# Rearranging the input half of an S4D + token-mixer kernel: block-diagonal input rows in one set, MLP modulations side by side, columns spread over steps 10 to 30

## The chip, the cores and the metric

The kernel runs on one core of one Trainium2 chip. The metric is device time in microseconds (us) of one execution: the median of several runs. One further execution was recorded by the hardware profiler, and all rows below come from it.

## The reference

Input `x` is 2048 tokens by 448 channels. A condition vector `c` gives six modulation vectors of 448 values; the block then is a long convolution (S4D) and a token-mixing MLP, each behind a layer norm:

```python
mod = (silu(c) @ w_mod).reshape(1, 6, 1, 448)
sa, ca, ga, sb, cb, gb = (mod[:, k] for k in range(6))
h = layernorm(x) * (1 + ca) + sa
K = 2 * einsum("dn,dnl->dl", C, exp(A * dt * l)).real        # 448 x 2048 kernel, 256 modes
y = irfft(rfft(h, 4096) * rfft(K, 4096))[:2048] + h * D_skip # along the tokens
x = x + ga * y
h = layernorm(x) * (1 + cb) + sb
x = x + gb * (gelu(layernorm(h).T @ w1 + b1) @ w2 + b2).T
```

## The kernel before, in words

TensorE (PE) computes everything that is a sum: the S4D kernel `K` from its 256 modes, the Fourier transforms as two-stage products with tables, and the MLP. ScalarE (ACT), VectorE (DVE) and GpSimd (POOL) feed it. The order of PE, ACT, DVE and POOL is the program's own order (manual schedule). The order of SyncE (SP), which issues most DMAs, is the program's only until `first.close()`, at step 8; after that a scheduler orders it.

**Steps and windows.** The S4D kernel is made in 56 steps `s` of half a group of 16 channels. In a step (`st_step`) ACT takes `ab`, three sines and cosines (L644 to L649), POOL makes two products `G` (L651, L652) and, two steps ahead, the tile `m` (L630, L632 in `st_mag2`), DVE four products `E` (L653 to L657), and PE the next phases (`st_phase`, L603) and 128 small products into `kg` (`st_kgen`, L678). A step is recognised in the trace by its `ab` (L644), and "step 8" below is the moment at which that instruction starts. Ahead of every eighth step stands a `window(s)`: logs and exponentials on ACT under another function table (`logs`, `angle`), with sixteen exponentials `mag` (L614). Eight steps and the window behind them are called a cycle: steps 0 to 8 the first cycle, 8 to 16 the second, and so on. From step 32 on the cycles carry only the generation and the products of the second half; at 422 us the MLP begins, whose matmuls fill PE to the end.

**What is hung into the steps.** Lists `dve` and `act` hold closures that are run at fixed points (`flush`), `late[s]` holds loads, and tables set how much of other work a step takes along:

- `u_stats(r)`: mean and variance of 128 tokens of x, sixteen times (L494, L495). `x_load` brings x in by POOL's DMA queue.
- `modulation(k, ...)`: one of the six modulation vectors, as four matmuls (L481) whose weights `w_mod` (784 KB each) were loaded before, copied out by ACT (L485). 1, 2 and 3 run in steps 2 to 7, 0 in the window of step 8, 4 and 5 in the window of step 16.
- `u_norm`, `u_rows(n)`: the first transform stage of x, "rows". 32 calls with two matmuls each out of 32 partitions into 64 columns (L525), one DVE product each by `mod[1]` (L528), and for every second call a DMA of 448 KB into `yu_d` (L530). They run in window 8, in steps 8 to 15 and in window 16. Tile `yt` has three buffers.
- `u_cols(k)`: the second stage, "columns". 32 calls with one matmul (L557) of what was read back from `yu_d` (L548), an output on DVE or ACT (L564, L566), and DMAs to `us_d`. They run from step 17 to 31.
- `chain(q)`, q = 1, 2, 3: elementwise work of 128 channels' parameters, cut into pieces by `yield`; `more(n)` runs n pieces. `pace` sets how many per step, `WPACE` how many per eighth of a window. A chain stops at `"logs"` until ACT has run `logs` in a window. Its results go to DRAM (`pars`, L378) and are read back by `load`.

Of the kernel before, what the change touches and what calls it, by code (L numbers as in the profile page):

```python
# [11 lines left out]
F32 = mybir.dt.float32  # L12
# [27 lines left out]
def dft_tables():  # L40
# [16 lines left out]
    t["WU"] = np.tile(w1.transpose(1, 2, 0).reshape(32, 64), (4, 1))  # L57
# [45 lines left out]
    t["S2"] = su.reshape(2, 4, 8, 2, 32 * P).transpose(3, 0, 2, 1, 4).reshape(P, 32 * P)  # L103
# [113 lines left out]
def tile_adaln_s4d_mixer(ctx, tc, i, out):  # L217
# [6 lines left out]
    yu_d = dram.tile([2, 32, 2, 8, 4, D], F32, name="yu_d")  # L224
    us_d = dram.tile([2, 32, P, DC], F32, name="us_d")
    v_d = dram.tile([32, P, D], F32, name="v_d")
    x2_d = dram.tile([L, D], F32, name="x2_d")

# [9 lines left out]
    with ExitStack() as es:  # L238
# [27 lines left out]
        def par_load(q):  # L266
            n = min(P, D - P * q)
            raws[q] = {}
            for nm in ("A_C_real", "A_C_imag", "A_log_A_real", "A_A_imag"):
                raws[q][nm] = qp.tile([P, N], F32, tag=nm, name=nm, bufs=2)  # L270
                nc.sync.dma_start(raws[q][nm][0:n], i[nm][P * q : P * q + n])
# [40 lines left out]
        wu = xp.tile([P, 64], F32, name="wu")  # L312
        wms = {}

        def wm_load(k, tile, eng=nc.sync):
            wms[k] = tile
            eng.dma_start(wms[k], i["w_mod"][:, k * D : (k + 1) * D].rearrange("(q p) d -> p q d", p=PP))
# [11 lines left out]
        def wm_slot(k):  # L329
            w = wm0.rearrange("p k d -> p (k d)")[0:PP]  # L330
            return w[:, 4 * D * (k % 4) : 4 * D * (k % 4 + 1)].rearrange("p (q d) -> p q d", q=4)

        late = {
            2: lambda: wm_load(2, wm_slot(2), G),
            3: lambda: wm_load(3, wm_slot(3), G),
            5: lambda: wm_load(0, wm_slot(0), G),
            6: lambda: [
# [3 lines left out]
            9: lambda: nc.sync.dma_start(svt, i["SV"]),  # L343
            10: lambda: [s2_load(0), s2_load(1)],
            11: lambda: [s2_load(2), s2_load(3)],
            12: lambda: wm_load(4, xt[0:PP, 0:4]),
            13: lambda: wm_load(5, xt[0:PP, 4:8]),
# [14 lines left out]

        def chain(q):

# [7 lines left out]
            def split(src, places):  # L372
                hl = qp.tile([P, 2, N], F32R, tag="hl", name="hl", bufs=3)[0:n]
                V.tensor_copy(hl[:, 0], src)
                yield
                tt(hl[:, 1], src, hl[:, 0].bitcast(F32), ALU.subtract)
                for k, v in places:
                    nc.sync.dma_start(pars[q][v, k, 0:n], hl.bitcast(F32))  # L378
# [25 lines left out]
            stt(s, t, -80 * math.log(2.0) / 2.0**80, s, ALU.mult, ALU.add)  # L404
            yield
            stt(s, ya, 0.5, s, ALU.mult, ALU.add)
            yield
            ts(s, s, ldt2[0:n, q : q + 1], None, ALU.add)
# [4 lines left out]
            ts(ph, aim, dt4[0:n, q : q + 1], None, ALU.mult)  # L413
            yield
            ts(u, ph, MAGIC, MAGIC, ALU.add, ALU.subtract)
            yield
            tt(ph, ph, u, ALU.subtract)
# [3 lines left out]
            ts(u, ph, 128.0, MAGIC, ALU.mult, ALU.add)  # L421
            yield
            ts(u, u, MAGIC, None, ALU.subtract)
            yield
            stt(p64, ph, 128.0, u, ALU.mult, ALU.subtract)
# [3 lines left out]
            ts(xa, xa, 4 * i2p, -0.5, ALU.mult, ALU.add)  # L429
            yield  # L430
            ts(u, cr, 0.0, 0.5, ALU.is_ge, ALU.subtract)
            yield
            tt(xa, xa, u, ALU.mult)
            yield
            ts(u, ci, 0.0, 0.5, ALU.is_ge, ALU.subtract)
            yield
            stt(xa, xa, 0.5, u, ALU.add, ALU.mult)
            yield
            stt(xa, ph, 63.0, xa, ALU.mult, ALU.add)
            yield  # L440
            ts(u, xa, MAGIC, MAGIC, ALU.add, ALU.subtract)
            yield
            tt(xa, xa, u, ALU.subtract)
            yield
            yield from split(xa, [(2, 0)])
        def logs(root=False):
# [7 lines left out]
            if root:  # L454
                S.activation(rs, mv[:, :, 1], AF.Ln, bias=eps_t)
                S.activation(rs, rs, AF.Exp, scale=-0.5)
# [19 lines left out]
        def modulation(k, *halves):  # L476
            if 0 in halves:
                pmods[k] = pms.tile([P, D], F32, tag="ms", name="pm")
            for h in halves:
                for q in (2 * h, 2 * h + 1):  # L480
                    T.matmul(pmods[k], scb[:, q], wms[k][:, q], start=q == 0, stop=q == 3)  # L481
            if 1 not in halves:
                return
            pm = pmods.pop(k)
            act.append(lambda: S.activation(mod[k], pm, AF.Copy, bias=1.0 if k in (1, 4) else 0.0))  # L485
# [11 lines left out]
        def u_scale():  # L497

            tt(nm, rs, rs, ALU.mult)
# [5 lines left out]
        yts = {}  # L505

        def u_norm(R):
            for r in (2 * R, 2 * R + 1):
                if R > 2:
                    S.activation(xt[:, r], xt[:, r], AF.Identity, bias=nm[:, r : r + 1], scale=rs[:, r : r + 1])  # L510
                    continue
                G.tensor_scalar(xt[:, r], xt[:, r], rs[:, r : r + 1], nm[:, r : r + 1], ALU.mult, ALU.add)

        def u_rows(n):

            R, g = divmod(n, 4)
            gp, gl = divmod(g, 2)
            if gl == 0:
                yts[R, gp] = xp.tile([P, 2, D], F32, tag="yt", name="yt", bufs=3)
            if g == 1 and 2 <= R < 7:  # L520
                act.append(lambda: u_norm(R + 1))
            pm = pms.tile([P, D], F32, tag="ms", name="pu")
# [841 lines left out]
```

## Time and profile before

| | |
|---|---|
| runs | 715.73, 719.15, 719.76 us; median 719.15 |
| profiled execution | 720.78 us, of which the trace's span is 719.0 |
| busy | PE 88%, DVE 63%, ACT 61%, POOL 38% of the span |
| mean granted TensorE clock | 0.921 |
| step 0, 8, 16, 24, 32 start at | 28.05, 98.48, 155.38, 205.67, 255.88 us |
| MLP | 422 us to the end |

Shares of busy time are averages over stages with different limits. PE is the bound of the MLP; in the stages before it no engine is full, and what counts there is which wait ends last in a step. The granted clock is read by stretch: 1.00 is full, 0.50 half speed, at which every matmul takes about twice as long.

### The profile page before, as it was taken

To read this page: it belongs to the slowest core of one execution; us is meant where nothing else is said; L and a number is where in the kernel's file an instruction comes from. 1 tells how busy PE (TensorE), PEld (TensorE's weight loads), DVE (VectorE), ACT (ScalarE), POOL (GpSimd) and SP (SyncE) were. 2 spreads that over 40 slices of the span, in tenths; PEclk is the share of its full clock that TensorE was granted. 3 is DMA by queue.
4 is the path that set the end of the run, shared out by engine and by line. 5 is a ranking of instruction groups with operands and counts; after the bars stand their busy time and mean duration, and the time that the engine had idled before them with its cause. 6 is when DMAs were issued, how large, how long until landed. Compare 5 with 4: busy or idle time off the path is not lost. (4 is left out here: it accounts for less than half of the span.)

```text
span 719.0 us, 18288 instructions
## 1 busy us (share of the span) xinstructions
PE 632.4 (88%) x7204; PEld 456.4 (63%) x7204; DVE 453.2 (63%) x875; ACT 438.7 (61%) x876; POOL 273.6 (38%) x328
## 2 busy tenths in 40 slices
PE   0659889979989888799888949999999999999997
PEld 0335335434535556566565617778999999999996
DVE  7469879679778668586684548778622263334441
ACT  5847588887987789989883549787522242222220
POOL 6486437528737787878785600000000000000000
PEclk9868857988998889999899959999999999999999
DMA  7795464266888635535236989974585436655540
GB/s 169 207 191 131 162 192 138 113 229 179 244 227 248 204 92 133 149 100 154 70 102 181 285 245 266 239 195 113 174 231 146 148 109 172 173 155 154 156 139 26
DMA packets 101635, 121.19 MB, mean 169 GB/s; under 512 B 13066, under 2 KB 87422, under 8 KB 101422
## 3 DMA queue, kind: packets, MB, share of 16 engines
q1 hardware_dynamic: 100014, 113.16, 55.2%
q0 software_dynamic: 1536, 6.87, 4.4%
q8 instruction: 57, 0.93, 0.6%
q14 instruction: 28, 0.23, 0.1%
HBM read 84.64 MB, written 34.87 MB: 166 GB/s over the span
## 5 line engine op out<-in xcount | busy, mean ns | idle before, releaser
L202 ACT CAST whi<-w 128x896 fp32r<-128x896 f32 x64 | 59.7, 938 | 131.4 <-PE o L1331 84.7
L651 POOL TENSOR_TENSOR G<-mag,gs 128x512 f32<-128x512 f32 x56 | 71.9, 1284 | 92.4 <-ACT gs L647 92.1
L211 DVE TENSOR_TENSOR wlo<-w,whi 128x896 fp32r<-128x896 f32 x64 | 68.0, 1087 | 40.3 <-ACT whi L202 31.0
L603 PE MATMUL xg<-tab,lph 64*128 64x512 f32 x112 | 68.8, 617 | 25.9 <-ACT xg L649 8.0
L1196 PE MATMUL acc<-h3h,whi 128*128 128x448 f32 x224 | 83.3, 372 | 0.1
L1197 PE MATMUL acc<-h3l,whi 128*128 128x448 f32 x224 | 81.9, 366 | 0.0
L1331 PE MATMUL o<-ul,whi 128*128 128x448 f32 x224 | 81.3, 363 | 0.0
L1330 PE MATMUL o<-uh,whi 128*128 128x448 f32 x224 | 81.2, 362 | 0.0
L1198 PE MATMUL acc<-h3h,wlo 128*128 128x448 f32 x224 | 80.9, 361 | 0.0
L1332 PE MATMUL o<-uh,wlo 128*128 128x448 f32 x224 | 80.6, 360 | 0.0
L678 PEld LDWEIGHTS kg<-E,G 128*32 128x32 f32 x3584 | 59.8, 119 | 32.3 <-issue 16.4
L603 PE MATMUL xe<-tab,lph 64*128 64x512 f32 x112 | 67.8, 609 | 12.2 <-ACT gs L648 10.2
L678 PE MATMUL kg<-E,G 128*32 128x64 f32 x3584 | 69.8, 235 | 2.2 <-issue 1.5
L652 POOL TENSOR_TENSOR G<-mag,gs 128x512 f32<-128x512 f32 x56 | 71.7, 1280 | 0.0
L653 DVE TENSOR_TENSOR E<-m,xe 128x512 f32<-128x512 f32 x56 | 38.3, 683 | 40.8 <-ACT xe L646 31.8
L632 POOL TENSOR_TENSOR m<-mag,w 128x512 f32<-128x512 f32 x56 | 59.9, 1070 | 6.0 <-DVE E L657 1.5
L1334 DVE SCALAR_TENSOR_TENSOR y<-o,b,mod 128x448 f32<-128x448 f32 x16 | 10.9, 684 | 80.3 <-PE o L1332 80.3
L644 ACT ACTIVATE ab<-xe 128x512 f32<-128x512 f32 x56 | 33.7, 601 | 30.3 <-PE xe L603 16.1
L1196 PEld LDWEIGHTS acc<-h3h,whi 128*128 128x128 f32 x224 | 42.3, 189 | 13.8 <-ACT h L1252 6.3
L603 PE MATMUL xe<-tab,lex 64*128 64x512 f32 x56 | 31.7, 575 | 18.8 <-POOL dsk L468 17.2
L614 ACT ACTIVATE mag<-xe 128x512 f32<-128x512 f32 x56 | 35.5, 634 | 19.7 <-PE xg L603 14.0
L603 PEld LDWEIGHTS xg<-tab,lph 64*128 64x128 f32 x112 | 24.3, 217 | 36.3 <-issue 10.3
(229 smaller groups left out, 1486.1 us busy)
## 6 DMA issues: line engine op xcount, KB each, us to landing
w<-in_B_w_dram SPq DMA_DIRECT2D x64, 224.0 KB
w<-in_B_w_dram SPq DMA_DIRECT2D x32, 448.0 KB
yu_d<-yt SPq DMA_DIRECT2D x16, 448.0 KB
yi<-yu_d SPq DMA_DIRECT2D x32, 224.0 KB
us_d<-uo SPq DMA_DIRECT2D x16, 448.0 KB
u<-us_d SPq DMA_DIRECT2D x32, 224.0 KB
v_d<-vt SPq DMA_DIRECT2D x32, 224.0 KB
vt<-v_d SPq DMA_DIRECT2D x16, 448.0 KB
```

The lines of the kernel that those rows point to most:

```text
L211: eng.tensor_tensor(lo, w, hi.bitcast(F32), ALU.subtract)
L603: T.matmul(out[k], lhs[r], rhs[r], start=start, stop=stop)
L632: G.tensor_tensor(m2, me, w[:, :, None].to_broadcast([P, GD, 32]), ALU.mult)
L651: G.tensor_tensor(Gt[:, 1], mg_, v32(sg), ALU.mult)
L652: G.tensor_tensor(Gt[:, 0], mg_, v32(cg_), ALU.mult)
L678: T.matmul(kgs[g][32 * q : 32 * q + 32, m], Gt[:, c, d], E[:, c, d], start=h == 0 and c == 0 and m == 0, stop=h == 1 and c == 1, skip_grou ...
L1196: nc.tensor.matmul(acc[f], hi[:, fs], h3h[:, r], start=r == 0, stop=False)
L1197: nc.tensor.matmul(acc[f], hi[:, fs], h3l[:, r], start=False, stop=False)
L1198: nc.tensor.matmul(acc[f], lo[:, fs], h3h[:, r], start=False, stop=r == 15)
L1330: nc.tensor.matmul(o, hi[:, ks], uh[kh][:, k], start=kh == 0 and k == 0, stop=False)
L1331: nc.tensor.matmul(o, hi[:, ks], ul[kh][:, k], start=False, stop=False)
L1332: nc.tensor.matmul(o, lo[:, ks], uh[kh][:, k], start=False, stop=kh == 1 and k == 6)
```

## The change

All of it lies ahead of the MLP. Line numbers of the changed kernel are about 30 higher (L603 is L633, L481 is L495, L525 is L556, L557 is L587, L678 is L708, L464 is L479, L651 is L681, L378 is L396).

1. Rows. The table `WU` becomes block diagonal, 128 by 128. `u_rows` is called 16 times, with two matmuls each out of 64 partitions into 128 columns; the DVE products stay 32, the DMAs 16. All run in window 8, nothing of them in the steps or in window 16. The first four `u_norm` are on DVE, the other twelve on ACT, six rows ahead.
2. Modulations. 1 and 2 are whole in steps 6 and 7, 0 in the window of step 8; 3, 4 and 5 are computed together in steps 27 and 30, each in 32 output columns, and spread over the partitions through DRAM (`mod_d`). `w_mod` for 1, 2 and 0 is loaded by SP in `late[5]`, no longer by SP and POOL at steps 0 to 5.
3. Columns: one each in steps 10 to 14, one or two in steps 16 to 22 and 24 to 30, three each in windows 16 and 24. `yu_d` is read from step 9 on; `us_d` is written for every second column.
4. Chains. The first half of chain 1 is in window 0, its second half in window 8 and on POOL (`fuse` splits a three-operand instruction in two). Windows take up to 32 pieces, steps at most two and none before step 10. All chains store to `pars` by POOL's queue. The parameters of chain 1 are loaded by ACT's queue at the start.
5. Statistics move one step and more back (step 3 takes one, steps 4 to 7 two, window 8 three). `first.close()` moves to step 16.

```diff
+    wu = np.zeros((2, 2, 32, 32, 2, 2))
+    for g in range(2):
+        wu[:, g, :, :, :, g] = w1.transpose(1, 2, 0)
+    t["WU"] = wu.reshape(P, P)
...
-            2: lambda: wm_load(2, wm_slot(2), G),
-            3: lambda: wm_load(3, wm_slot(3), G),
-            5: lambda: wm_load(0, wm_slot(0), G),
+            5: lambda: [
+                wm_whole(1),
+                wm_whole(2),
+                wm_whole(0),
...
+            late_eng = G if q == 1 else V
...
-                    nc.sync.dma_start(pars[q][v, k, 0:n], hl.bitcast(F32))
+                    G.dma_start(pars[q][v, k, 0:n], hl.bitcast(F32))
...
+        def u_rows(r):
+
+            R, o = divmod(r, 2)
+            yt = xp.tile([P, 2, D], F32, tag="yt", name="yt", bufs=3)
+            pm = [pms.tile([P, D], F32, tag="ms", name="pu") for _ in range(2)]
+            for g in range(2):
+                p = slice(64 * g, 64 * g + 64)
+                T.matmul(pm[g], wu[p], xt[p, r], start=True, stop=True)
+
+            def out(g):
+                tt(yt[:, g], pm[g], mod[1], ALU.mult)
+                if g:
+                    nc.sync.dma_start(yu_d[o, :, :, :, R].rearrange("k c a g d -> (k c a) (g d)"), yt.rearrange("p g d -> p (g d)"))
...
-            if s in (8, 16):
-                for k in (0,) if s == 8 else (4, 5):
-                    modulation(k, 0, 1)
...
-                if s in (8, 16):
-                    some(u_rows, rows, (2, 2, 2, 2, 2, 0, 1, 1)[e])
-                elif s == 24 and e != 5:
+                if s == 8 and e == 3:
+                    for h in range(2):
+                        mod_whole(0, h)
+                if s == 8 and e == 1:
+                    u_scale()
+                    for r in range(4):
+                        u_norm(r)
+                    act.extend([partial(u_norm, 4), partial(u_norm, 5)])
+                elif s == 8 and e:
+                    some(u_rows, rows, 3 if 2 < e < 7 else 2)
+                elif s in (16, 24) and e in (2, 4, 7):
                     some(u_cols, cols, 1)
...
-        pace = [2] * 32
+        pace = [0] * 10 + [1, 1, 1, 1, 2, 2] + [1] * 16
+        share = {s: 1 for s in range(10, 15)} | {s: 1 + s % 2 for s in range(16, 23)} | {s: 2 - s % 2 for s in range(24, 31)}
...
-                if 2 <= s < BATCH:
-                    for r in range(2 * s, 2 * s + 2):
+                if 3 <= s < BATCH:
+                    for r in range(*((4, 5, 7, 9, 11, 13)[s - 3 : s - 1])):
...
-            if 1 < s < 8:
-                modulation(s // 2, s % 2)
+            if s in (6, 7):
+                for h in range(2):
+                    mod_whole(s - 5, h)
+                if s == 7:
+                    flush(act)
```

PE's order from step 7 into window 8, before (the group `lex` holds the exponents' weights, `pm` a modulation, `pu` rows):

```order
L678 MATMUL kg<-E,G 32x64 x32
L603 MATMUL xe<-tab,lex_145 128x512
L603 MATMUL xg<-tab,lex_145 128x512
L481 MATMUL pm<-wm_79,scb 128x448 x6
L603 MATMUL xe<-tab,lex_145 128x512
L603 MATMUL xg<-tab,lex_145 128x512
L678 MATMUL kg<-E,G 32x64 x32
L525 MATMUL pu<-xt,wu 64x448 x4
```

And now, from the last phase of step 7 on:

```order
L495 MATMUL pm<-wm_80,scb 128x448 x4
L708 MATMUL kg<-E,G 32x64 x32
L633 MATMUL xe<-tab,lex_146 128x512
L633 MATMUL xg<-tab,lex_146 128x512
L495 MATMUL pm<-wm_80,scb 128x448 x4
L633 MATMUL xe<-tab,lex_146 128x512
L633 MATMUL xg<-tab,lex_146 128x512
L708 MATMUL kg<-E,G 32x64 x32
```

Two whole modulations stand ahead of the window's second pair of exponents, where half of one and a whole one stood between the first and the second pair. The first rows (not shown) follow two more pairs of exponents and one more `kg` than before.

ACT's order at the same place, before and then now (`mod_...` are modulations, `xa<-ya` is the window's first instruction):

```order
L649 ACTIVATE xg<-ab 128x512
L692 COPY ks<-kg 128x256
L464 ACTIVATE xa<-ya 128x256
L449 ACT_TABLE_LOAD
L451 ACTIVATE u<-ya 128x256
```

```order
L679 ACTIVATE xg<-ab 128x512
L498 ACTIVATE mod_106<-pm 128x448
L722 COPY ks<-kg 128x256
L498 ACTIVATE mod_107<-pm 128x448
L479 ACTIVATE xa<-ya 128x256
L467 ACT_TABLE_LOAD
```

The copy of the second modulation now stands ahead of the window's first instruction.

POOL's order in window 8, before (the last `G` of step 7, normalisations of x, two `m`, the first `G` of step 8) and then its start now:

```order
L652 TENSOR_TENSOR G<-mag,gs 128x512
L512 TENSOR_SCALAR xt<-xt,rs,nm 128x448 x4
L630 TENSOR_TENSOR w<-mag 128x16
L632 TENSOR_TENSOR m_991<-mag,w 128x512
L512 TENSOR_SCALAR xt<-xt,rs,nm 128x448 x2
L630 TENSOR_TENSOR w<-mag 128x16
L632 TENSOR_TENSOR m_1055<-mag,w 128x512
L651 TENSOR_TENSOR G<-mag,gs 128x512
```

```order
L682 TENSOR_TENSOR G<-mag,gs 128x512
L392 CAST hl<-A_log_A_real 128x256
L394 TENSOR_TENSOR hl<-A_log_A_real,hl 128x256
L396 DMA pars_58<-hl 128x512 x2
L660 TENSOR_TENSOR w<-mag 128x16
L662 TENSOR_TENSOR m_965<-mag,w 128x512
L376 TENSOR_SCALAR t<-t 128x256
L377 TENSOR_TENSOR s<-t,s 128x256
L376 TENSOR_SCALAR u<-u 128x256
L377 TENSOR_TENSOR s<-u,s 128x256
L426 TENSOR_SCALAR s<-s,ldt_173 128x256
```

In place of six normalisations POOL has 32 instructions and 6 DMA issues of chain 1 between `G` of step 7 and `G` of step 8.

More of the change, by code (lines that the diff above doesn't have):

```diff
@@ L361, in flush, with fuse @@
                 todo.pop(0)()
+        def fuse(eng, out, a, c, b, op0, op1):
+            if eng is V:
+                stt(out, a, c, b, op0, op1)
+                return
+            part = a if out is b else out
+            eng.tensor_scalar(part, a, c, None, op0)
+            eng.tensor_tensor(out, part, b, op1)
         def chain(q):
+            late_eng = G if q == 1 else V
             n = min(P, D - P * q)
@@ L503, in u_scale @@
             stt(nm, mv[:, :, 0], -1.0, rs, ALU.mult, ALU.mult)
[L505 to L522, printed above, removed]
-            p = slice(32 * g, 32 * g + 32)
-            for o in range(2):
-                T.matmul(pm[64 * o : 64 * o + 64], wu[p], xt[p, 2 * R + o], start=True, stop=True)
-            def out():
-                tt(yts[R, gp][:, gl], pm, mod[1], ALU.mult)
-                if gl:
-                    nc.sync.dma_start(
-                        yu_d[:, :, :, R, 2 * gp : 2 * gp + 2].rearrange("o k c g d -> (o k c) (g d)"),
-                        yts.pop((R, gp)).rearrange("p g d -> p (g d)"),
-                    )
-            dve.append(out)
@@ L940, in more @@
                     return
-        rows, cols, pieces = iter(range(32)), iter(range(32)), [0, 0]
+        rows, cols, pieces = iter(range(16)), iter(range(32)), [0, 0]
         def some(f, it, n):
@@ L990, in window @@
                 mellow()
-                if s == 8 and e == 0:
-                    tt(mod[1], mod[1], mod[2], ALU.mult)
                 flush(dve)
```

186 lines of the change are left out of this document (107 added, 79 removed).

## The prediction

> **What bounds the kernel now.** I read the busy time by stretch first, cut at the cycles, then at steps and windows, then the timelines around the longest gaps. A row has the stretch, its length, the busy time of PE, weight loads, DVE, ACT and POOL with their instructions, the granted clock, the DMA share and GB/s.
>
> ```profile
> 28.05:98.48 70.43, 55.10 (x733) 27.22 (x732) 55.41 (x112) 42.62 (x87) 41.52 (x49) 0.75 0.69 178
> 98.48:155.38 56.90, 52.77 (x886) 27.98 (x886) 44.92 (x87) 47.30 (x92) 30.67 (x32) 0.83 0.42 146
> 155.38:205.67 50.29, 42.52 (x757) 22.52 (x755) 42.99 (x78) 42.51 (x85) 30.89 (x32) 0.90 0.77 214
> 205.67:255.88 50.21, 44.44 (x758) 25.28 (x758) 37.16 (x64) 39.96 (x78) 36.89 (x42) 0.86 0.73 215
> 255.88:299.68 43.80, 37.90 (x804) 25.15 (x802) 30.34 (x54) 39.89 (x84) 34.62 (x39) 0.92 0.51 133
> 422.00:719.00 297.00, 289.55 (x1408) 254.77 (x1404) 146.89 (x299) 118.59 (x204) 0.00 (x0) 0.98 0.61 166
> ```
>
> The MLP is PE's and untouched. Cycles one to four take 70.43, 56.90, 50.29 and 50.21 us, while the fifth, which carries no rows, columns or modulations, takes 43.80. What the change can reach is the excess of these four, first that of the first two.
>
> ```profile
> 68.12:98.48 30.36, 27.96 (x342) 12.26 (x344) 25.14 (x61) 18.78 (x38) 11.07 (x13) 0.75 0.56 185
> 98.48:130.93 32.45, 29.93 (x496) 15.41 (x496) 27.75 (x46) 28.93 (x56) 24.02 (x25) 0.76 0.44 144
> 130.93:155.38 24.45, 22.84 (x392) 12.57 (x390) 17.18 (x42) 18.37 (x37) 6.64 (x8) 0.93 0.41 149
> 155.38:186.45 31.07, 24.65 (x397) 12.84 (x396) 28.77 (x48) 25.90 (x51) 24.57 (x26) 0.84 0.70 189
> 186.45:205.67 19.22, 17.87 (x361) 9.67 (x361) 14.22 (x31) 16.61 (x34) 6.31 (x7) 1.00 0.89 255
> 239.20:255.88 16.68, 15.15 (x355) 10.28 (x354) 9.07 (x17) 13.31 (x26) 11.80 (x17) 0.80 0.56 167
> 255.88:284.87 28.99, 23.96 (x516) 15.65 (x518) 22.03 (x40) 25.30 (x54) 22.03 (x21) 0.88 0.46 113
> ```
>
> Rows one, three, five and six run from the last step ahead of window 8, 16, 24, 32 to the first one behind it; rows two, four and seven are the steps 8 to 15, 16 to 23, 32 to 39. In windows 8 and 16 PE is busy nearly throughout (27.96 of 30.36, 22.84 of 24.45): PE bounds them.
>
> **The first steps.** Timeline of POOL, DVE, ACT, PE; in brackets the idle time ahead and what ended it:
>
> ```profile
> 30.20 1.27 POOL L651 TENSOR_TENSOR G<-mag,gs 128x512 f32<-128x512 f32 x1 [8.48 <-ACT gs L647]
> 38.50 2.00 POOL L292 DMA_DIRECT2D xt<-in_A_u_dram  x4
> 45.85 0.63 DVE L494 BATCH_NORM_STATS2 st<-xt 128x6 f32<-128x448 f32 x1 [5.53 <-DMA xt<-in_A_u_dram]
> 51.45 0.76 PE L603 MATMUL xg<-tab,lph 64*128 64x512 f32 x1 [7.87 <-issue]
> 53.19 0.60 ACT L644 ACTIVATE ab<-xe 128x512 f32<-128x512 f32 x1 [7.35 <-PE xe L603]
> 70.28 1.29 POOL L651 TENSOR_TENSOR G<-mag,gs 128x512 f32<-128x512 f32 x1 [1.33 <-ACT gs L647]
> 174.92 0.60 ACT L644 ACTIVATE ab<-xe 128x512 f32<-128x512 f32 x1
> 186.45 0.60 ACT L644 ACTIVATE ab<-xe 128x512 f32<-128x512 f32 x1 [0.28 <-PE xg L603]
> ```
>
> DVE stands 5.53 us before a statistic whose x has not landed; the products E behind it come late, PE idles 7.87 us, and step 4 begins only at 53.19. Without such stalls three steps (the last two rows, steps 20 to 23) take 11.53 us, 3.84 each. Now this statistic is asked for a step later, and the loads of `w_mod` no longer compete with x this early. POOL's first G starts at 30.20; seven steps at 3.84 and two x loads of 2.00 put G of step 7 at 61.1 instead of 70.28, and step 6 prepares no `m` (below: 1.3), so 59.8: 10.5 earlier. The 784 KB loads now start together while the last x is still coming, and step 5 asks for the first of it; I charge 2 for that. **Term 1: step 7 8.4 earlier** (10.5 if all has landed, 2 if the transfers still set the pace).
>
> **Window 8.** PE and DVE and ACT rows, the first three at full clock, the fourth at half:
>
> ```profile
> 71.12 4.78 PE L481 MATMUL pm<-wm,scb 112*128 112x448 f32 x12
> 79.99 0.98 PE L525 MATMUL pu<-xt,wu 32*64 32x448 f32 x8
> 135.84 1.16 PE L716 MATMUL y<-wc,ks 64*64 64x64 f32 x62 [0.21 <-DVE yt L528]
> 87.10 1.77 PE L525 MATMUL pu<-xt,wu 32*64 32x448 f32 x8
> 78.53 0.49 PE L603 MATMUL xe<-tab,lex 64*128 64x512 f32 x1
> 88.91 1.15 DVE L528 TENSOR_TENSOR yt<-pu,mod 128x448 f32<-128x448 f32 x2 [0.23 <-PE pu L525]
> 71.38 0.44 ACT L464 ACTIVATE xa<-ya 128x256 f32<-128x256 f32 x1
> 74.90 0.57 ACT L614 ACTIVATE mag<-xe 128x512 f32<-128x512 f32 x1
> 77.29 1.32 PE L525 MATMUL pu<-xt,wu 32*64 32x448 f32 x8
> ```
>
> A matmul of a modulation is 0.8 (six in 4.78, two records each), a modulation 3.2. From the start of step 7 (68.12 before; all offsets count from there) PE now has modulation 1, kg (1.1, estimated from L716's 62 here), a pair of exponents (0.5) and modulation 2: 8.0 us, begun 0.2 before. ACT's copy of modulation 2 (0.6, as its 0.57 for a `mag`) stands ahead of the window's first instruction, so that starts at 8.4, not 3.3. Between it and the first `mag` lay 3.5, of which some 0.5 (two tiny instructions for the layer norm) moves behind the second pair: `mag` at 11.4 instead of 6.8. Four `mag` at about 0.5 (1.9), these 0.5, then the scale factors and a normalisation on DVE (1.5; the same lay between 74.90 and 77.29 before) follow, and rows start at 15.3 instead of 9.2 (77.29). This is the cost of whole modulations and late statistics.
>
> Then, until the phase of step 8: 14 of the 16 rows (the last two stand behind it). A new row does what eight records of L525 did, 0.95; the block-diagonal halves lie in different row groups, as L603's pairs do, which run together. So 13.3, modulation 0 3.2, four pairs of exponents 1.8, L716 1.2, the phase 1.3 (an estimate: two such pairs and shorter ones between): 20.8. DVE's 28 products at 0.57 take 16 and hide in that. The clock:
>
> ```profile
> 82.30:84.70 2.40, 0.01 (x1) 0.01 (x2) 2.37 (x5) 0.21 (x1) 1.25 (x2) 0.75 0.60 211
> 84.70:103.90 19.20, 19.20 (x180) 7.88 (x180) 13.68 (x35) 12.00 (x22) 1.86 (x2) 0.50 0.62 210
> 107.50:117.30 9.80, 9.80 (x152) 5.45 (x154) 9.77 (x16) 7.60 (x15) 7.74 (x9) 0.50 0.24 69
> 86.00:97.00 11.00, 11.00 (x98) 4.27 (x98) 9.20 (x25) 6.61 (x12) 0.00 (x0) 0.50 0.92 312
> ```
>
> After 2.40 us without PE work the clock fell to 0.50 and stayed there for 19.20 us in which PE was never idle; a second such stretch lasted 9.80. Now PE, done with `kg` of step 6, waits some 2 to 3 us for `mag`, so I expect a cold start of the rows. How long it lasts is the open size: if all 20.8 run at half, they take 20.8 more. The rows of before used half of the array at a time; the new ones use all of it. I take 6 us of half clock, 3 lost.
>
> The Trainium skill, "TensorE: Matmul & The Clock Gate", Part 1, has the clock fall after an idle window of about 3.4 us and return after some 3.4 us of sustained work. The fall agrees within the window's phase; the return does not, since 19.20 fully busy us did not bring it back. By that rule 1.7 would be lost, and the sum below would be 1.3 lower.
>
> The DMAs bound it from another side: 14 rows of 448 KB and six stores of 256 KB are 8.0 MB, at 312 GB/s (last row above) 25.6. So the window ends at 15.3+24 to 26: **Term 2: 40.0 instead of 30.36, 9.6 later.** Low end 36 (full clock), high end 57.
>
> POOL's share: 32 instructions and six stores of chain 1, in place of normalisations.
>
> ```profile
> 75.75 3.13 POOL L512 TENSOR_SCALAR xt<-xt,rs,nm 128x448 f32<-128x448 f32 x4 [2.95 <-DVE nm L503]
> 80.19 1.87 POOL L512 TENSOR_SCALAR xt<-xt,rs,nm 128x448 f32<-128x448 f32 x2
> 79.16 1.05 POOL L632 TENSOR_TENSOR m<-mag,w 128x512 f32<-128x512 f32 x1
> 13.23 0.72 POOL L835 TENSOR_TENSOR wm<-ph,wm 128x256 fp32r<-128x256 f32 x1
> ```
>
> At 0.72 for two operands and about 0.5 for one (448 columns take 0.78) they make some 20, the stores 3 (0.5 each, as L292's), two `m` 2.6 (1.05 and 0.24): 26 from 12 on, done at 38, ahead of G of step 8 at 42. So it costs nothing; DVE's 0.4 us pieces that it replaces lay in a PE-bound window. But the same L512 took 0.94 instead of 0.78 each at 80.19, while DVE worked on SBUF: at that rate 5 more, done at 43, 1 late. The Trainium skill, "SBUF — State Buffer", section "Who interferes with whom", lets the two block each other at a shared port only if DVE has two SBUF inputs or a two-port mode. By it the rows' products, one input of which lies in PSUM, would leave POOL alone, and nothing is late; no run here shows it.
>
> **Cycle 2.** Steps 8 to 15 lose 15 of the 32 old rows and half of the chain pieces, gain five columns. They took 32.45 with 9.80 of it at half clock; steps 32 to 39 take 28.99. I take 29.0 (27 if POOL's 3.84 alone counts, 31.07 as steps 16 to 23): 3.5 less. Window 16 loses two modulations (6.4) and its rows, gains three columns and keeps its chain: 17.0, between windows 32 (16.68) and 24 (19.22, seven columns): 7.5 less. **Term 3: 11.0** (7 to 13).
>
> **Cycles 3 and 4.** Steps 16 to 23 no longer open with the first reads of `yu_d`, which I hold for the reason that they took 31.07: 29.0. Window 24 has three columns instead of seven but more chain pieces: 19.2 to 17.0. In cycle 4 four columns fewer stand against 12 matmuls of modulations (3.2 if three run side by side, 9.6 if not): 0, between -2 and 3. **Term 4: 4.3** (0 to 6).
>
> Loading chain 1's parameters before step 0 can delay the first exponents by up to 1; bringing them forward frees SP later. I take nothing. Three `mod` tiles through DRAM have until the MLP.
>
> **The sum.** -8.4 + 9.6 - 11.0 - 4.3 = -14.1. The profiled execution took 720.78 (span 719.0), 1.63 above the median 719.15; from the median the sum gives 705.
>
> **The rivals.**
>
> - *Cold rows (slower).* PE stays at half clock from the rows' start to the end of window 8, as it did for 19.20 us. The window then takes 57, not 40: 17 more; and if the steps behind it begin cold as well, like the 9.80 us above, they lose the 3.5 of term 3: -14.1+17+3.5 = +6.4, 726. It turns the sign from 14 us of further loss on. For it: both stretches above; against: the fuller array. 0.10. The clock gate's page speaks against it with its 3.4 us.
> - *The DMA ring.* `yt` has three buffers; if a row takes 2.6 until its buffer is free again, 14 take 37: 12 more than now, 717. Before, writes followed each other at 1.4 (below). 0.09.
>
> ```profile
> 90.09 2.77 SPq L530 DMA_DIRECT2D yu_d<-yt  x2
> 118.03 5.26 SPq L530 DMA_DIRECT2D yu_d<-yt  x2
> ```
>
> - *No gain in the first steps.* The transfers of x and `w_mod` are as many bytes up to 60 us as before, less one 784 KB; if they set the pace, step 7 comes 2 earlier instead of 8.4: 711.5. 0.17.
> - *Warm window.* PE keeps its clock and the DMAs keep up: 36, 701; with the low ends of cycles 2 and 3, 697. 0.16.
>
> The forecast has the remaining 0.48, with 701 to 709 its own range.
>
> **How the numbers follow.** About 0.5%, 3.6 us, is what a measurement of this kernel can tell from no change. Forecast, warm window and the third rival are faster: 0.48+0.16+0.17 = 0.81. The ring is no change: 0.09. Cold rows are slower: 0.10. The range 696 to 719 leaves out the cold rows (0.10) and what errors of the terms may carry beyond its ends.
>
> **What would show it.** Step 7 at 58 to 62, step 8 at 98 to 102, step 16 at 144 to 148, step 24 at 190 to 194, then the old spacing. Wrong if step 8 is later than 108 with a clock of 0.50 through window 8 (cold rows), if DVE's products wait on `yu_d` writes, if G of step 8 starts late behind chain 1, or if steps 8 to 15 still take 32.

## The result: slower by 1.25%

The kernel after takes 724.64 us (median of 14 runs, 721.71 to 727.74), the kernel before 716.36 beside it (14 runs, 710.65 to 721.21): a ratio of 1.0125, 95% interval 1.0102 to 1.0149. The forecast was 705, faster. The median of the kernel before shifts a little between groups of runs (713.69 to 716.36), so the runs below are compared by their ratio to the kernel before measured with them. The ratios and their intervals leave out the few executions in a slower state of the chip, so they are not exactly the quotients of the medians.

The same stretches as in the prediction, for the kernel after: cycles one to five, then step 7 to step 8 (window 8), steps 8 to 15, window 16, steps 16 to 23, windows 24 and 32 (start and end, length, busy time of PE, weight loads, DVE, ACT, POOL, granted clock, DMA share, GB/s):

```profile
28.82:111.96 83.14, 63.69 (x737) 34.88 (x735) 51.43 (x102) 48.57 (x95) 61.01 (x78) 0.82 0.56 167
111.96:162.45 50.49, 41.62 (x809) 24.65 (x805) 42.71 (x77) 42.06 (x85) 34.51 (x39) 0.86 0.64 185
162.45:210.11 47.66, 39.13 (x747) 21.56 (x745) 43.35 (x79) 41.56 (x85) 34.18 (x38) 0.93 0.80 217
210.11:257.58 47.47, 41.62 (x781) 22.95 (x782) 32.58 (x59) 40.10 (x78) 37.13 (x45) 0.93 0.72 212
257.58:300.20 42.62, 36.80 (x804) 24.69 (x800) 28.93 (x52) 39.88 (x83) 34.46 (x38) 0.96 0.48 130
56.98:111.96 54.98, 43.56 (x363) 22.41 (x363) 29.98 (x62) 26.19 (x50) 35.50 (x47) 0.78 0.54 179
111.96:142.93 30.97, 24.88 (x457) 14.08 (x453) 23.76 (x38) 25.42 (x51) 23.96 (x27) 0.89 0.70 200
142.93:162.45 19.52, 16.74 (x353) 10.57 (x352) 18.94 (x40) 16.64 (x35) 10.55 (x13) 0.83 0.55 163
162.45:193.93 31.48, 25.03 (x397) 12.92 (x396) 27.73 (x45) 26.47 (x54) 25.55 (x27) 0.89 0.82 228
193.93:210.11 16.18, 14.10 (x351) 8.64 (x351) 15.62 (x36) 15.08 (x32) 8.63 (x12) 1.00 0.76 197
236.63:257.58 20.95, 17.02 (x372) 10.54 (x368) 10.55 (x20) 13.94 (x26) 14.80 (x21) 0.84 0.66 208
```

Step 7 comes 11.1 earlier (56.98 instead of 68.12), and step 8 comes 13.5 later: window 8 takes 54.98 instead of 30.36. The cycles behind it win most of that back: at step 40 this profile is 0.5 behind the profile that the prediction used (300.20 against 299.68), and 5.3 behind a second profile of the kernel before (294.88; that run is below). SP's loads ahead of window 8 and its timeline, in order, with lines left out (in brackets the idle time ahead and its cause):

```profile
44.19 5.28 SPq L619 DMA_DIRECT2D lex<-pars  x1
50.07 5.97 SPq L337 DMA_DIRECT2D wm<-in_w_mod_dram  x3
...
64.43 5.53 PE L495 MATMUL pm<-wm,scb 112*128 112x448 f32 x8 [7.32 <-DMA wm<-in_w_mod_dram]
78.76 0.49 PE L633 MATMUL xe<-tab,lex 64*128 64x512 f32 x1 [2.68 <-ACT mag L644]
83.19 3.69 PE L556 MATMUL pu<-xt,wu 64*128 64x448 f32 x7 [0.56 <-DVE xt L545]
87.98 5.70 PE L495 MATMUL pm<-wm,scb 112*128 112x448 f32 x8
116.91 1.11 PE L556 MATMUL pu<-xt,wu 64*128 64x448 f32 x1 [3.58 <-DVE yt L559]
```

PE stands idle for 7.32 us ahead of modulation 1: its `w_mod` is asked for only at 50.07, behind a load of `lex` that keeps SP's queue for 5.28, and has not landed. Modulation 1 then runs at half clock (5.53 instead of 3.2). After the next wait, 2.68 for ACT's `mag`, the first rows and modulation 0 (5.70) run at half clock as well. Behind the phase of step 8 the last two rows wait 3.58 for PSUM that DVE frees late. Where the transfers went shows in the busy time by stretch, first of the kernel before from 28 to 36 us:

```profile
28.00:36.00 8.00, 2.98 (x15) 1.66 (x12) 5.45 (x9) 6.74 (x15) 5.71 (x8) 0.77 0.86 204
```

SP's load in it, from the timeline of the kernel before:

```profile
29.36 0.43 SPq L317 DMA_DIRECT2D wm<-in_w_mod_dram  x1
```

And the kernel after in the same time, during PE's wait, behind it, and from the first row until the clock is back:

```profile
28.00:36.00 8.00, 5.75 (x47) 3.04 (x47) 6.85 (x15) 7.91 (x16) 4.95 (x7) 1.00 0.11 35
56.98:64.60 7.62, 0.30 (x2) 0.17 (x2) 7.12 (x16) 3.18 (x6) 5.66 (x5) 0.62 1.07 246
79.00:92.00 13.00, 12.44 (x84) 6.31 (x84) 6.62 (x14) 7.69 (x16) 11.61 (x17) 0.51 0.34 132
83.19:92.90 9.71, 9.71 (x17) 4.54 (x18) 4.25 (x8) 4.03 (x8) 8.71 (x13) 0.50 0.31 123
```

Before, the DMAs were at 0.86 from 28 to 36 us, with the first `w_mod` asked for at 29.36; now they are at 0.11 there, and full (1.07) some 25 us later with PE waiting. (A load of x is part of the difference: POOL asks for it at 32.64 before and at 34.73 now.)

### The profile page after: what moved, and what is told of

Same layout as the page of the kernel before. It is cut to its first block, busy times and chain, and to the rows that moved or that the text cites. A ratio compares the mean times of both kernels' runs of the same rounds, so it can differ in the third digit from the quotient of the medians.

```text
span 721.3 us, 18223 instructions
## 1 busy us (share of the span) xinstructions
PE 623.1 (86%) x7140; PEld 457.6 (63%) x7140; DVE 446.2 (62%) x852; ACT 438.3 (61%) x876; POOL 300.2 (42%) x371
## 5 line engine op out<-in xcount | busy, mean ns | idle before, releaser
L681 POOL TENSOR_TENSOR G<-mag,gs 128x512 f32<-128x512 f32 x56 | 71.9, 1285 | 39.5 <-ACT gs L677 39.4
L633 PE MATMUL xg<-tab,lph 64*128 64x512 f32 x112 | 67.7, 606 | 16.4 <-DVE E L687 5.4
L708 PEld LDWEIGHTS kg<-E,G 128*32 128x32 f32 x3584 | 59.1, 119 | 33.3 <-issue 19.9
L633 PE MATMUL xe<-tab,lph 64*128 64x512 f32 x112 | 66.7, 598 | 11.7 <-ACT gs L678 9.1
L708 PE MATMUL kg<-E,G 128*32 128x64 f32 x3584 | 69.0, 234 | 6.8 <-ACT ks L722 4.2
L633 PE MATMUL xe<-tab,lex 64*128 64x512 f32 x56 | 31.9, 581 | 16.0 <-DMA lex<-wm 11.5
L1365 PEld LDWEIGHTS o<-uh,whi 128*128 128x128 f32 x224 | 42.1, 188 | 3.1
L1233 PEld LDWEIGHTS acc<-h3h,wlo 128*128 128x128 f32 x224 | 42.1, 188 | 3.0
```

The costliest lines, as they stand in the source:

```text
L633: T.matmul(out[k], lhs[r], rhs[r], start=start, stop=stop)
L681: G.tensor_tensor(Gt[:, 1], mg_, v32(sg), ALU.mult)
L708: T.matmul(kgs[g][32 * q : 32 * q + 32, m], Gt[:, c, d], E[:, c, d], start=h == 0 and c == 0 and m == 0, stop=h == 1 and c == 1, skip_grou ...
L1233: nc.tensor.matmul(acc[f], lo[:, fs], h3h[:, r], start=False, stop=r == 15)
L1365: nc.tensor.matmul(o, hi[:, ks], uh[kh][:, k], start=kh == 0 and k == 0, stop=False)
```

## The experiments

The theory is that window 8 is long because `w_mod` is asked for too late, in time in which the DMAs are full, and because PE's gaps cost half clock behind them. The rivals: the bytes of x and `w_mod` set the pace wherever they are asked for; the rows themselves (their price, DVE, PSUM) are the cost; or POOL's chain 1 is. Times of steps and windows are from each run's profiled execution.

**w_mod early** (diffs here and below are shortened; `...` marks what is left out).

```diff
         late = {
+            2: lambda: wm_whole(2, G),
             5: lambda: [
-                wm_whole(1),
-                wm_whole(2),
-                wm_whole(0),
+                wm_whole(0, G),
...
             load(g, False)
+        wm_whole(1)
         remainder()
```

> The kernel after, but w_mod is loaded as before the change (modulation 1's part by SP behind the first chain, 2 and 0 by POOL at steps 2 and 5). Theory W (the wait for w_mod makes window 8 long): PE's 7.32 us wait ahead of modulation 1 goes, with it part of the half clock behind it; window 8 takes 42 to 48 us instead of 54.98 and the whole 4 to 9 us less than the kernel after. Rival X (the bytes set the pace): the early loads delay x and the statistics by as much, step 7 starts 6 to 10 us later than 56.98, step 8 stays at 110 to 113 and the time is that of the kernel after within 2 us. Rival R (price and clock of the rows): the gap goes, but the rows run at half clock all the same, window 8 still takes over 50 us.

721.53 us, ratio 1.0085 (1.0053 to 1.0117), against 1.0125. Window 8 is 47.03, 8 shorter, and PE's wait for `w_mod` is gone, as theory W says. But step 7 comes at 62.50, 5.5 later, because a statistic now waits for x:

```profile
58.65 0.63 DVE L529 BATCH_NORM_STATS2 st<-xt 128x6 f32<-128x448 f32 x1 [4.19 <-DMA xt<-in_A_u_dram]
```

Step 8 is only 2.4 earlier (109.53). Theory W and rival X are both partly right: the wait was real, and most of it moved to x. Rival R is right that the rows still run at half clock (0.56 from 75 to 90 us), and wrong on the window, which it kept over 50.

**Early w_mod, and the halves of modulations 1 and 2 early** (`if 1 < s < 6: mod_whole(s // 2, s % 2)`).

> As the run with early w_mod, and modulations 1 and 2 are made in halves in steps 2 to 5 as before the change, so that the window's ACT is not held by the copy of modulation 2. Theory W: a further 4 to 6 us off step 8 (the two modulations, 6.4 us of PE work, leave the path between step 7 and the first mag); step 8 at 98 to 103, the whole 8 to 14 us less than the kernel after, which is at or under the kernel before. Rival R: step 8 not before 107, the whole within 4 us of the kernel after.

722.82, ratio 1.0098 (1.007 to 1.0127). Window 8 is 38.57, near the 40.0 forecast, but steps 5 to 6 take 16.2:

```profile
60.12 3.36 PE L494 MATMUL pm<-wm,scb 112*128 112x448 f32 x4 [10.79 <-DMA wm<-in_w_mod_dram]
```

Step 8 stays at 109.40, where theory W had 98 to 103. Computing with these bytes earlier only moves the wait to an earlier step: theory W's further gain is refuted, and its rival's bounds hold.

**The last two rows ahead of the phase** (row table 4, 3, 3, 3, 3).

> The kernel after with its row table 4,3,3,3,3 and none in the last slot, so that the last two rows no longer stand behind the phase of step 8. Theory: PE's wait of 3.58 us and the half clock behind it (117 to 123) go; step 8 to 9 takes 4 to 5 us instead of 8.22, window 8 is 0 to 1.5 longer, the whole 2 to 4 us less. Rival: the two rows cost the same ahead of the phase (window 8 gets longer by 3 or more), the time is that of the kernel after within 1.5 us.

722.82, ratio 1.0085 (1.0051 to 1.0119), against 1.0125. From step 8 to 9 it takes 4.52 instead of 8.22, window 8 only 0.4 more. The theory holds for this place. For the whole the ratios give about 3 us, near the size of the intervals, and the profile does not show it: window 24 takes 18.39 instead of 16.18, and step 40 comes at 300.61, as in the kernel after (300.20).

**All three, and modulations 3 to 5 through POOL's queue.**

> Early w_mod, halves in steps 2 to 5, the two rows ahead of the phase, and the row of modulations 3 to 5 goes through DRAM by POOL's queue instead of SP's, so that the loads of SI at step 32 do not stand behind it. Theory: the three gains add (10 to 16 us less than the kernel after), window 32 takes 17 to 18 instead of 20.95: 706 to 712, under the kernel before. Rival: later windows give the gain back (SP's loads set the pace from step 16 on), the whole within 5 us of the kernel after.

718.33, ratio 1.0028 (1.0004 to 1.0053): 7 us of the 9 are back, more than the rival allowed and less than the theory's 10 to 16. Step 8 is at 113.60 (PE waits 13.28 for `w_mod` at step 5), so the gain lies behind it: steps 8 to 15 take 27.92 instead of 30.97, window 32 takes 17.92 instead of 20.95.

**The kernel before again.**

> The kernel before, once more, to see which of its stages vary between executions (its profiled execution of 720.78 lies 4.9 above the median 715.91 of 30 runs). Theory S: the stall at step 4 (12.9 us from step 3 to step 4, while x had not landed) is not in every execution; an execution near the median has step 7 at 60 to 64 instead of 68.12 and keeps that up to step 8. Rival C: step 7 is at 67 to 69 again and the difference lies in stretches of half clock behind it.

715.17, ratio 0.9997. Its profile has a span of 713.9, where the one that the prediction used has 719.0. The rows are window 8, cycle 2, steps 8 to 15 and window 16.

```profile
67.69:97.68 29.99, 27.61 (x342) 12.36 (x344) 25.00 (x61) 18.78 (x39) 11.02 (x13) 0.80 0.55 186
97.68:152.08 54.40, 50.17 (x885) 26.16 (x885) 43.67 (x84) 46.77 (x91) 30.63 (x32) 0.89 0.43 153
97.68:128.50 30.82, 28.10 (x494) 14.47 (x496) 27.30 (x46) 28.74 (x55) 23.98 (x25) 0.81 0.45 153
128.50:152.08 23.58, 22.07 (x393) 11.70 (x389) 16.37 (x39) 18.03 (x36) 6.65 (x8) 1.00 0.41 153
```

Rival C is right: step 7 is at 67.69 again, the stall at step 4 stays. Cycle 2 took 54.40 instead of 56.90, at a clock of 0.89 instead of 0.83: part of what the prediction saw to be won in cycle 2 was half clock that this second execution does not have.

**Rows spread** (8 rows in window 8, one in each of steps 8 to 15; columns from step 17).

> The kernel after, but only 8 of the 16 rows stand in window 8, the others one to each of steps 8 to 15, and the columns follow from step 17 as before the change (2 to a step, 7 in window 24, then 3). Late statistics, whole modulations, w_mod at step 5 and the MLP modulations side by side stay. Theory P (too much in one window): window 8 takes 44 to 47 us instead of 54.98 (6 rows at 1.28 and less waiting on DVE), steps 8 to 15 take 31 to 33, and by step 32 2 to 5 us of it are left. Rival Z (the rows cost the same wherever they stand): what window 8 gains the steps 8 to 31 give back; the whole within 2 us of the kernel after.

730.61, ratio 1.0200 (1.0154 to 1.0246): slower still. Window 8 is 44.77, as theory P says, but steps 8 to 15 take 38.10, where it had 31 to 33. PE is idle from 107 to 117, by the busy time of that stretch:

```profile
107.00:117.00 10.00, 0.00 (x0) 0.00 (x0) 3.17 (x6) 3.85 (x9) 9.13 (x12) 0.59 0.07 26
```

The timeline has the reason:

```profile
113.60 1.28 POOL L681 TENSOR_TENSOR G<-mag,gs 128x512 f32<-128x512 f32 x1
114.92 0.60 ACT L677 ACTIVATE gs<-xg 128x512 f32<-128x512 f32 x1 [6.12 <-POOL G L681]
```

G of step 8 stands behind chain 1 on POOL, and ACT's `gs` behind G. This gap is not the whole loss: cycles 3 and 4, where the columns now stand two and three to a step, take 52.10 and 54.02 instead of 47.66 and 47.47. On the whole time theory P and rival Z both fail.

**x earlier** (with early `w_mod`; the first line added stands at the end of window 0).

```diff
                 S.activation(one, one, AF.Sin)
+                x_load(4, 4, G)
...
-            if s < 2:
-                x_load(4 + 4 * s, 4 + 4 * s, G)
+            if s == 0:
+                x_load(8, 8, G)
```

> The kernel after with the w_mod loads as before the change and, beyond that, the two x loads of POOL one step earlier (into POOL's and the DMAs' idle time at 22 to 36 us). Theory X (the bytes set the pace up to step 8): with the idle DMA time used, the statistic no longer waits for x (4.19 us in the run with early w_mod alone), step 7 at 56 to 58, window 8 at 45 to 47, step 8 at 102 to 105, the whole 3 to 6 us less than the run with early w_mod (721.53). Rival L: x delays the loads of the first exponents and step 0 starts 3 or more later than 28.8, nothing is gained.

717.66, ratio 1.0023 (0.9989 to 1.0057), 4 us under early `w_mod` alone. Window 8 is 45.58. Step 7 is at 60.80 (expected 56 to 58) and step 8 at 106.38 (expected 102 to 105), so theory X is right in kind and not in full; step 0 starts at 29.02, so rival L is out. The DMAs now work at 0.82 from 20 to 28 us, where they were at 0.61 with early `w_mod` alone. This run differs from the kernel after only in when, and by which queue, `w_mod` and x are asked for, and 7 of the 9 us are back.

**x earlier and all the rest** (halves of modulations 1 and 2 in steps 4 to 7, the rows ahead, POOL's queue).

> As the run with earlier x, with modulations 1 and 2 in halves in steps 4 to 7, the last two rows ahead of the phase, and the row of modulations 3 to 5 through POOL's queue. Theory: the gains add: step 8 at 100 to 104, window 32 at 17 to 18, 708 to 714, under the kernel before (715.91). Rival: the later windows take longer as soon as step 8 comes earlier (as in the run of all three, whose window 24 began only 1 us ahead of the kernel after): 716 to 719.

712.91 (706.91 to 719.08), ratio 0.9942 (0.9907 to 0.9978): faster than both kernels, as the theory says. Window 8, cycle 2, steps 8 to 15, window 32:

```profile
60.46:102.74 42.28, 38.41 (x364) 20.79 (x365) 31.05 (x63) 25.48 (x48) 32.95 (x45) 0.88 0.57 215
102.74:150.44 47.70, 39.58 (x800) 23.70 (x796) 40.09 (x69) 42.09 (x84) 33.98 (x38) 0.86 0.74 205
102.74:130.69 27.95, 22.74 (x448) 13.06 (x444) 22.40 (x34) 25.45 (x51) 23.91 (x26) 0.88 0.78 210
224.93:240.13 15.20, 14.53 (x372) 8.99 (x368) 10.02 (x20) 13.76 (x26) 11.47 (x16) 1.00 0.72 218
```

POOL's timeline around step 8 (102.74):

```profile
101.95 0.61 POOL L395 DMA_DIRECT2D pars<-hl  x1 [0.30 <-POOL hl L393]
106.32 1.27 POOL L680 TENSOR_TENSOR G<-mag,gs 128x512 f32<-128x512 f32 x1 [3.76 <-ACT gs L676]
```

No long wait for `w_mod` is left; POOL's chain ends 3.8 us ahead of its G. The profiled execution (706.91) is the fastest of its runs, 6 us under their median, so the rows above show this version at its best.

**The kernel before with single parts.** x earlier; and the change's statistics:

> The kernel before with one edit: its two x loads of POOL one step earlier. Theory X (bytes of x set the first steps): the 12.2 us from step 3 to step 4 shrink to 5 to 8, step 8 at 91 to 94 instead of 97.7 and the time is 3 to 6 us under the kernel before: then most of what the change's late statistics bring is to be had without it. Rival: step 8 stays within 2 us of 97.7 (w_mod's bytes, issued at steps 2 and 3 in both, are what is late), the time within 0.4%.

> The kernel before with one edit: the statistics in the change's table (two rows at step 3 and so on, the last three ahead of window 8), all loads as they were. Theory (term 1 of the prediction alone): step 4 no longer waits for x and comes 5 to 8 earlier, step 7 at 60 to 63 instead of 67.7. Rival: a modulation's half, whose w_mod is late too, takes the place of the statistic in PE's queue; step 7 within 3 us of 67.7.

715.12, ratio 1.0014 (0.9989 to 1.0038), and 723.27, ratio 1.0128 (1.0088 to 1.0168). One row of the first, on PE's wait:

```profile
53.13 3.35 PE L481 MATMUL pm<-wm,scb 112*128 112x448 f32 x4 [12.06 <-DMA wm<-in_w_mod_dram]
```

And of the second:

```profile
59.75 3.35 PE L481 MATMUL pm<-wm,scb 112*128 112x448 f32 x4 [12.03 <-DMA wm<-in_w_mod_dram]
```

In the first run x no longer stalls DVE, and PE waits 12.06 for `w_mod` in the same place. The rival is right on `w_mod` and on the time, not on step 8, which comes at 100.97, 3.3 later. In the second run step 4 comes at 45.25, 8 earlier, as term 1 says, and step 6 gives it all back (step 7 at 70.60): the rival is right. Late statistics alone make the kernel before as slow as the whole change does (1.0128 and 1.0125); this run does not show where all of that comes from.

**Chain 1 on DVE** (`late_eng = V`), with spread rows and in the fastest version:

> The run of spread rows (730.61), with the late part of chain 1 on DVE instead of POOL. Theory G (POOL's chain 1 is the next bound behind window 8: there it ended at 113.6 while G of step 8 was wanted at 107, and PE stood idle from 107 to 117): the gap goes, steps 8 to 15 take 31 to 33 instead of 38.1, the whole 4 to 8 us less than 730.61. Rival: DVE's 20 pieces in window 8 lengthen it by as much; 728 or more.

> The run with earlier x and all edits (712.91), with the late part of chain 1 on DVE. Theory G: there POOL ended its chain at 102.6 and G of step 8 was wanted at 106.3, so POOL is not the bound and DVE, with 20 us of row products in the window, is the worse place: 0 to 4 us slower. Rival: POOL's port or its stores delayed the window; 1 to 3 us faster.

729.27, ratio 1.0211 (1.0177 to 1.0244), and 714.41, ratio 1.0001 (0.9967 to 1.0036). With spread rows PE's wait in the gap falls from 11.03 to 4.81, and steps 8 to 15 take 31.81 instead of 38.10: POOL's chain was their bound. The whole does not show it (window 8 is 3.0 longer, and cycles 3 and 4 stay at 52.56 and 53.87), so theory G holds for the place, not for the time. In the fastest version DVE is the worse place by 0.6% of the ratio, with intervals that just overlap; window 8 takes 45.14 instead of 42.28.

**PE kept busy in the two gaps** (nine matmuls ahead of modulation 1, four behind modulation 2).

> The kernel after with PE kept busy in its two gaps: nine matmuls of 0.8 us ahead of modulation 1 (into its own PSUM tile, overwritten by its first real matmul) and four behind modulation 2 (into a tile that nobody reads). No wait is taken away. Theory K (a part of window 8's length is the cold clock behind the gaps: 59 to 68 and 79 to 92 us at 0.50): the clock stays at 1.0, modulation 1 takes 3.3 instead of 5.53 us, modulation 0 3.3 instead of 5.70, the rows from 83 to 92 run at full clock; window 8 is 6 to 10 shorter, step 8 at 102 to 106, the whole 4 to 8 less than the kernel after. Rival D (the rows wait on DVE's products and three PSUM slots, not on PE's clock): window 8 less than 3 shorter, the whole within 2 us.

724.33, ratio 1.0138 (1.0088 to 1.0188). Its timeline: the filler, modulation 1, the four records of the first row's two matmuls (two records each, overlapping), then the two of the third matmul, which has no partner yet.

```profile
58.29 9.18 PE L495 MATMUL pm<-xt,scb 112*128 112x448 f32 x18
67.31 3.17 PE L497 MATMUL pm<-wm,scb 112*128 112x448 f32 x8
83.72 1.02 PE L558 MATMUL pu<-xt,wu 64*128 64x448 f32 x4 [1.98 <-DVE xt L547]
84.58 0.91 PE L558 MATMUL pu<-xt,wu 64*128 64x448 f32 x2
```

And the stretch that ran at 0.51 above:

```profile
79.00:92.00 13.00, 10.36 (x137) 5.18 (x125) 6.78 (x15) 9.48 (x20) 11.61 (x17) 1.00 0.32 125
```

The clock stays up, modulation 1 takes 3.17, and window 8 takes 50.73, 4.2 less, where theory K had 6 to 10 and rival D less than 3. The 4.2 is what is left after the filler's own cost: it starts at half clock and holds modulation 1 until 67.31, 2.9 later than in the kernel after, so half clock itself may have been worth more. The whole gains nothing that can be measured, as rival D says; by step 32 the profile is 1.9 ahead of the kernel after, by step 47 0.2. The first row's two matmuls take 1.02 together and one alone 0.91, so they do run side by side. Even so the stretch from the first row to step 8 takes 25.05 (83.72 to 108.77) at full clock.

**Modulations 3 to 5 through POOL's queue** (`G.dma_start` for the row and its three copies).

> The kernel after with the row of modulations 3 to 5 going to DRAM and back by POOL's queue instead of SP's. Theory Q (on SP the loads of SI for window 32 stand behind these four transfers, PE waits 3.48 us for SI and then runs at half clock): window 32 takes 16 to 18 instead of 20.95, the whole 3 to 5 us less than the kernel after. Rival: the SI loads wait for their own buffers; window 32 stays over 20.

720.65, ratio 1.0089 (1.0057 to 1.0122), against 1.0125. Its window 32:

```profile
239.98:255.40 15.42, 14.77 (x370) 9.02 (x364) 10.70 (x19) 13.82 (x26) 11.59 (x16) 1.00 0.59 179
```

What PE met there in the kernel after:

```profile
251.22 1.76 PE L802 MATMUL kx<-yk,si 128*64 128x224 f32 x8 [3.48 <-DMA si<-in_SI_dram]
```

Window 32 takes 15.42, 5.5 less, and PE's wait for SI is gone: theory Q is right on the place. But the next load on SP, `t`, now makes PE wait right behind that window, and cycle 5 takes 45.16 instead of 42.62:

```profile
260.24 0.74 PE L828 MATMUL vv<-zy,t 64*128 64x224 f32 x1 [3.44 <-DMA t<-in_T_dram]
```

The ratios leave 2.6 us at the end, less than the theory's 3 to 5, and their intervals overlap.

**The first steps of the kernel before in order.**

> The kernel before with its first steps put in order: x loads of POOL one step earlier, statistics in the change's table, and the halves of modulations 1, 2, 3 in steps 4 to 7 instead of 2 to 7. Nothing else of the change. Theory F (what the version with all edits gains over the kernel before, 712.91 to 715.46, lies in these steps): step 7 at 58 to 61 instead of 67.7, no wait for w_mod, step 8 at 88 to 93, the whole 706 to 711. Rival M (the rows, columns and chain of the change carry that gain in cycles 2 to 4): the first steps gain as much but it is given back in cycles 2 to 4, as in the run of late statistics; 713 or more.

718.85, ratio 1.0043 (1.0004 to 1.0081): no gain. `w_mod` makes PE wait no more, but a load of 64 KB on SP does. It was asked for at 42.22, and the DMAs work at 0.98 to 1.09 of their time from 36 to 52 us:

```profile
61.91 0.76 PE L603 MATMUL xg<-tab,lph 64*128 64x512 f32 x1 [6.55 <-DMA lph<-pars]
```

Step 7 comes at 70.20. Theory F falls: the first steps are no faster for it. Nor does the fastest version's gain over the kernel before lie there: its step 8 comes at 102.74, 5.1 later than in the second profile of the kernel before (97.68), and its cycles 2 and 4 take 47.70 and 41.71 instead of 54.40 and 49.53.

## Why the prediction was wrong, point by point

- **Term 1 (step 7 earlier): right in kind, and beyond its upper end.** 11.1 instead of 8.4, where the end was 10.5. The 2 us charged for competing loads were put in the wrong place: step 7 no longer needs `w_mod`, so the debt fell due behind it.
- **Term 2 (window 8: 40.0): the step that failed.** It began the two modulations right at step 7 and had no term for the wait for their data (the 2 us in term 1 were the only charge). Of the 15 us that are missing, 7.3 are that wait and 2.3 modulation 1 at half clock: the first `mag` comes at +21.2 instead of +11.4, rows at +26.2 instead of +15.3. From there it took 28.8 instead of 24 to 26. The 3 us charged for half clock were not far off: the filler run, at full clock, takes 25.05 for this stretch, 3.7 less, though half clock lasted 9.7 us and not 6. What was too low is the 20.8 at full clock. The 0.95 for a row is about right (the filler run has 1.02, with the next matmul starting 0.86 after the first), but DVE's two products for a row take 1.16 and PE has three PSUM tiles ahead of them, so DVE probably sets the pace of the rows; no run isolates this. POOL's chain took 33.7 (78.29 to 111.98) instead of 26, since its one-operand instructions took 0.40 to 1.09 and not about 0.5. It cost nothing only because the window was longer still; with spread rows PE stood idle for 10 behind it, and moving it took 6.3 off steps 8 to 15.
- **Term 3 (cycle 2: -11.0): half.** It measured -6.4 against the profile used, -3.9 against the second one. Steps 8 to 15 took 30.97 instead of 29.0, with 8.2 for step 8 alone (the wait of the two rows behind the phase was not foreseen); window 16 took 19.52 instead of 17.0.
- **Term 4 (-4.3): the sum near (-5.4), its parts not.** Cycle 3 gave 2.6 instead of 4.3, cycle 4 2.7 instead of 0 (by the second profile 1.8 and 2.1). Steps 16 to 23 did not shorten (31.48), though the first reads of `yu_d` are gone from them: these were not what held them, or not alone. What does is not shown. Behind window 16 of the kernel after ACT loads a table, and PE waits twice for ACT's sines; the kernel before has the same pair (in the second fence):

```profile
163.67 1.28 ACT L676 ACT_TABLE_LOAD   x1
167.04 0.47 PE L633 MATMUL xe<-tab,lph 64*128 64x512 f32 x1 [2.10 <-ACT gs L678]
170.21 0.76 PE L633 MATMUL xg<-tab,lph 64*128 64x512 f32 x1 [2.70 <-ACT gs L678]
```

```profile
159.85 0.76 PE L603 MATMUL xe<-tab,lph 64*128 64x512 f32 x1 [3.56 <-ACT gs L648]
163.47 0.76 PE L603 MATMUL xg<-tab,lph 64*128 64x512 f32 x1 [2.86 <-ACT xg L649]
```

  In cycle 4 steps 24 to 31 gained 7.0, and window 32 lost 4.3 to the transfers of the late modulations on SP's queue.
- **The sum and its base.** Added up as the prediction adds them, the four terms measure -11.1 + 24.6 - 6.4 - 5.4 = +1.7 instead of -14.1; 15.0 of these 15.8 us are term 2, and the other three nearly cancel. Against the second profile of the kernel before they are +6.5. The execution that the prediction used lies 4.4 above the median of its 14 runs; more runs would have shown that.
- **The clock.** The prediction read the clock as falling after the gap of 2.40 us and called this in agreement with the rule that it cites. Its own row (82.30 to 84.70, a mean of 0.75) says that the clock fell half-way, some 1.2 us after PE's last matmul; that does not agree.
- **The rivals.** 726 for cold rows is close to the time by luck: half clock held for some 13 us, not to the end of the window, and the clock over the whole window was 0.78. The DMA ring is out: in window 8 DVE waits once for a write to `yu_d`, 0.34 us. "No gain in the first steps" had the right mechanism, bytes that set the pace, but looked for it ahead of step 7.

Shown by runs: the late `w_mod` and the move of its wait to x, the wait of the rows behind the phase, POOL's chain as the bound with spread rows, SP's queue at window 32. Open: why nothing of the filler run's 4.2 is left at the end, what sets the pace of the rows at full clock, and how the versions' gains divide over cycles 2 to 4, where two profiles of the same kernel differ by 2.5 us in cycle 2 at clocks of 0.83 and 0.89.

## What to carry to other kernels

When an operation is moved to a later place, look for when its data are asked for and what else the DMAs carry then: idle transfer time that is given up early (0.86 to 0.11 here) comes back as a wait later. A stall whose bytes set the pace is not removed by moving its reader; it goes to the next reader, as `w_mod` and x showed in five of the runs above, and `si` and `t` in a sixth. What helped was to ask for the bytes in time in which the DMAs were idle. And a "hidden" chain is hidden only for the window's length: price its end, not its place.

## What the runs showed of the hardware

The granted clock came back late: from the first row on PE was busy for all of 9.71 us at 0.50, and for 12.44 of 13.00 us from 79 to 92 at 0.51. The Trainium skill, "TensorE: Matmul & The Clock Gate", Part 1, has it return after some 3.4 us of sustained work; these rows do not agree. In the filler run, whose longest gap from 79 to 92 us is 1.98 us, the clock stayed at 1.00.

The two matmuls of a row, in different row halves of the array, run side by side: 1.02 us for both, 0.91 for one alone, at full clock.

With the DMAs at 0.98 to 1.09 of their time from 36 to 52 us, a load of 64 KB that was asked for at 42.22 still made PE wait until 61.91 (the last run above).
